# Halves of k and v that add up in the DMA, weight forms at other places, and another order in the opening of a pooled-attention and mixture-of-experts kernel

## The chip, the core and the metric

The kernel runs on one core of one Trainium2 chip. The metric is the device time of one execution in microseconds (us). The kernel before was run eight times: median 503.4, lowest 502.52, highest 504.22. The engines are named as in the profile: PE is TensorE's matmul and PEld its weight load, DVE is VectorE, ACT is ScalarE, POOL is GpSimd, SP is SyncE.

## The reference

```python
# B, H, S, D = 8, 8, 576, 64; q, k, v: [B, H, S, D]
k_p = k.reshape(B, H, 72, 8, D).mean(axis=3)
v_p = v.reshape(B, H, 72, 8, D).mean(axis=3)
attn = softmax(q @ k_p.T / sqrt(D))          # [B, H, S, 72]
x = (attn @ v_p) as [B * S, H * D]           # 4608 tokens x 512
p = domain_probs / domain_probs.sum(-1)      # 4608 x 4
for e in range(4):                           # w1[e]: 512 x 1024, w2[e]: 1024 x 512
    out += p[:, e:e + 1] * (relu(x @ w1[e]) @ w2[e])
```

Inputs and output are f32; the kernel computes in bf16 and sums in f32.

## The kernel before

The tokens are cut into nine chunks. Chunk `c` from 0 to 7 holds the first 512 tokens of batch `c`, in four rows of 128 (a token is `4 p + r` with partition `p` and row `r`); chunk 8 holds the last 64 tokens of all eight batches. Each chunk passes through four experts, so there are 36 steps (c, e), counted by `s`. A step's up product (hidden values, into `H_sb`) runs beside the down product of the step before (into `acc`). Every engine's instructions stand in the order in which the code issues them (`manual_schedule`); nothing reorders them. SP issues the DMA transposes and the stores, POOL all loads. Since an engine works its list from the top, an instruction that waits holds all behind it.

**Forms.** A 2 x 2 block product is made of seven products instead of eight, in the up products from step 2 on (but for step 4) and in the down products from (1, 0) to (8, 2). It needs sums and differences of blocks: `combine_w1` makes those of w1 (L621 to L624) and `combine_w2` those of w2 (L656 to L659, three into `w2_t`, profile name `w_t`, each from the one before, and one in place), four each for an expert; `forms_of` makes four of the chunk's input (L637, L641, `xf`), and `sums_of` four of the hidden values (L733 to L736, `h_s`; the last on POOL). They are additions of 128 x 1024 or 128 x 512 bf16 elements from SBUF to SBUF, on DVE except where a call names `nc.gpsimd`. `relu_sum` (L716) and `add` (L774) read PSUM on DVE; `relu` (L719), `keep` (L712) and the copies L811 and L827 are ACT's. `product` (L668) and `half_of` (L790) are PE's up and down products with forms, `up_half` (L699), `up_plain` (L686; its ReLU on ACT is L690) and `down` (L884) those without. Step 4, the first of chunk 1, is `up_plain` for all eight pieces, with `sums_of` behind it.

**Placing.** `point()` counts places in the order of work and runs what stands in `placed` under its count; `slot()` takes the next piece of `forms_due` and then calls `point()`. Forms of weights stand in `forms_due` by step, with `nothing` for free slots. Attention of batch 1 stands at points 41 to 69 (`second_attention`, within chunk 0), that of batch `b = c + 1` at points of chunk `c` (`attention(c)`).

**Keys and values.** 72 partitions hold 8 rows of 64 for each of 8 heads; they are folded to one row by additions. Batches 1 and 2 are loaded whole (`load_k`, `load_v`, by `load_kv`, L88), k into `raw_kv`, v into the part of `w2_t` that belongs to experts 2 and 3; folding takes a first addition of 4 rows (L222 in `first` for batch 2), one of 2 rows (L227) and a last one (L230; two for keys, to `kp`). From batch 3 on they come as two halves of four rows into `raw_kv` (`load_half`, L95): the second half is added to the first by the DMA, and so it may be issued only when the first has landed; the first addition falls away. `pool_waits` (L252) is a one-element copy on POOL that holds POOL's list until its operand is there; it is set ahead of a load that overwrites what DVE still reads.

**Opening.** Loads are issued as k, half of q0 (rows 0 and 1), v, the other half of q0, w1(0), w2(0) and so on. In `attention_first` PE pools k and v by matmuls (`first_keys`, `first_values`), transposes q (`first_queries`), takes scores (`first_scores`), the context of a pair of rows and half of the heads at a time (`context_first` and `divide`, L393 and L394), and turns it into `xT` (`turn_first`). `warm(n)` issues n matmuls on zeros whose result nobody reads. `attention_rest` places rows 2 and 3 between the first `up_half`s.

**Loads up to 90 us, in POOL's order.** ..., w1(3), w2(2) whole (two DMAs), q(1) as two halves of heads, v(1), w2(3), q_rem(0), q_rem(1); at point 43 k(2), at 52 q(2) and q_rem(2); at point 60 `pool_waits` on the folded v(1), then v(2) and the four forms of w2(1) on POOL:

```python
placed.setdefault(60, []).extend(
    [lambda: pool_waits(vps[1][0:1, H - 1, 0:1]), lambda: load_v(2)]
    + combine_w2(1, nc.gpsimd))
```

The forms of w2(2) stand in `forms_due` of steps 5 and 6 (two in each), those of w2(3) in steps 6 and 7 (one and three). Forms of w2(2) and w2(3) can't be made before v(2) has been folded, since the raw v lies in their place.

Of the kernel before, what the change touches and what calls it, by code (L numbers as in the profile page):

```python
# [18 lines left out]
def kernel(  # L19
# [99 lines left out]
    def load_first_q(half):  # L119
        if half == 0:  # L120
            raws[("q", 0)] = qpool.tile([P, H, NR, D], BF16, name="q_sb")
        nc.gpsimd.dma_start(
            out=raws[("q", 0)][:, :, 2 * half:2 * half + 2, :],
            in_=q[0, :, 0:NT, :].rearrange("h (p r) d -> p h r d", r=NR)[:, :, 2 * half:2 * half + 2],
        )

    def load_q_halves(b):
        raws[("q", b)] = qpool.tile([P, H, NR, D], BF16, name="q_sb")
        for hs in halves:
            nc.gpsimd.dma_start(  # L130
                out=raws[("q", b)][:, hs].rearrange("p h r d -> p h (r d)"),
                in_=q[b, hs, 0:NT, :].rearrange("h (p r) d -> p h (r d)", r=NR),
            )
# [24 lines left out]

    def load_w2(e):
        rows = moe_w2[e].rearrange("(fc p) d -> p fc d", p=P)  # L160
        for lo in (0, FCH // 2):
            fcs = slice(lo, lo + FCH // 2)
            nc.gpsimd.dma_start(out=w2_bf[:, e, fcs], in_=rows[:, fcs])
# [54 lines left out]
    def fold_parts(nm, b, hs, last, engine):  # L218

        def first():  # L220
            raw = raws[(nm, b)]
            engine.tensor_add(out=raw[:, hs, 0:4, :], in0=raw[:, hs, 0:4, :],  # L222
                                 in1=raw[:, hs, 4:8, :])

# [7 lines left out]
        return [first, rest] if b == 2 else [rest]  # L232
# [75 lines left out]
    def first_queries(half):  # L308
        if half == 0:
            state[("qT", 0)] = apool.tile([P, H, 2, P], BF16, name="qT", bufs=1)  # L310
        for g in range(2):
            qt_ps = psum_o.tile([P, 2, 2, P], BF16, tag="o_ps", name="qt_ps")
            for i in range(2):
                h = 2 * (2 * g + i)
                for rr in range(2):
                    for hh in range(2):
                        nc.tensor.transpose(
                            qt_ps[hh * D:(hh + 1) * D, i, rr, :],
                            raws[("q", 0)][:, h + hh, 2 * half + rr, :], ident[:],
                        )  # L320
            copy = nc.scalar.copy if half else nc.vector.tensor_copy
            copy(out=state[("qT", 0)][:, 4 * g + half:4 * g + 4:2], in_=qt_ps[:])
# [21 lines left out]
    def first_scores(half, g):  # L344
        kpT, qT = state[("kpT", 0)], state[("qT", 0)]
        if (half, g) == (0, 0):
            new_exp(0)
        apart = g == 1
        if apart:
            pool, tag = ((psum_h, "h_ps"), (psum_o, "o_ps"))[half]  # L350
            each = [pool.tile([P, NT], F32, tag=tag, name="one") for _ in range(2)]
            each = [bank[:] for bank in each]
        else:
            two = two_banks()
            each = [two[:, hh] for hh in range(2)]
        for i in range(2):
            pair = 2 * g + i
            for hh in range(2):
                lo = hh * D
                nc.tensor.matmul(  # L360
                    each[hh][0:SP, i * TH:(i + 1) * TH], lhsT=kpT[lo:lo + D, 2 * pair, 0:SP],
                    rhs=qT[lo:lo + D, 2 * pair + half].rearrange("c r p -> c (r p)"),
                )
        dst = state[("expT", 0)][:, 4 * g:4 * g + 4, half].rearrange(
            "j (i h) s p -> j h i (s p)", h=2)
        if apart:
            for hh in range(2):
                nc.scalar.activation(
                    out=dst[:, hh], in_=each[hh][0:SP].rearrange("j (i n) -> j i n", i=2),
                    func=ACT.Exp, scale=EXP_SCALE)  # L370
        else:
            nc.scalar.activation(
                out=dst, in_=two[0:SP].rearrange("j h (i n) -> j h i n", i=2),
                func=ACT.Exp, scale=EXP_SCALE)
# [15 lines left out]
    def divide(banks, x_tok):  # L390
        c_ps = banks[:, :, 0:NPAIR * (D + 1)].rearrange("p a (h d) -> p a h d", h=NPAIR)
        inv = npool.tile([P, 2, NPAIR], F32, name="inv")
        nc.vector.reciprocal(out=inv[:], in_=c_ps[:, :, :, D])  # L393
        nc.vector.tensor_tensor(  # L394
            out=x_tok, in0=c_ps[:, :, :, 0:D],
            in1=inv[:].unsqueeze(3).to_broadcast([P, 2, NPAIR, D]), op=ALU.mult,
# [19 lines left out]
    def context_first(t, half):  # L416
        x_tok = h_s[:, t].rearrange("p a n -> p (a n)").rearrange(
            "p (r a h d) -> p r a h d", r=2, a=2, h=NPAIR)
        banks = two_banks()
        for rr in range(2):  # L420
            context_half(0, 2 * t + rr, half, banks[:, rr])
        divide(banks, x_tok[:, :, half])
# [9 lines left out]
    def turn_first(t, half):  # L432
# [8 lines left out]
        copy = nc.vector.tensor_copy if half else nc.scalar.copy  # L441
# [61 lines left out]
    def attention_first():  # L503
# [5 lines left out]
        warm(1)  # L509
        first_queries(0)  # L510
        warm(1)
        first_scores(0, 0)
        warm(1)
        first_scores(0, 1)
        warm(1)
        first_values(0)
        warm(1)
        context_first(0, 0)
# [585 lines left out]
```

The softmax here doesn't subtract the row's maximum and nothing guards it: scores larger than these inputs give would overflow.

## Time and profile before

| | us |
|---|---|
| median of eight runs | 503.4 |
| the profiled execution | 503.38 |
| its span in the profile | 501.7 |
| PE busy | 490.8 (98% of the span) |
| DVE busy | 362.0 (72%) |
| ACT busy | 290.0 (58%) |
| POOL busy | 196.2 (39%) |
| moved by DMA | 41.90 MB, mean 84 GB/s |

The span goes from the first to the last instruction of one profiled execution; the device time contains 1.68 us more. In the lines below L12 is line 12 of the kernel; `out<-in` are the program's names of tiles, followed by partitions x elements. In lines of single instructions the first number is the start in us from the start of the span, the second the duration, and the bracket tells how long the engine had stood idle and what released it. PE's busy time includes `warm` and the pipelining of matmuls, so a busy PE need not be doing needed work.

### The profile page before, as it was taken

How to read it: one execution, taken by the hardware profiler on the slowest of the kernel's cores; microseconds unless marked ns; L12 is line 12 of the kernel's file. 1: busy time of each engine (PE TensorE's matmuls, PEld its weight loads, DVE VectorE, ACT ScalarE, POOL GpSimd, SP SyncE). 2: the span in 40 equal slices, each digit the busy share in tenths (PEclk: the TensorE clock that was granted, in tenths of full speed). 3: DMA queues.
4: the chain of work that ended last, by engine and by line, in shares of the span. 5: the costliest groups of instructions: out<-in, count | busy, mean ns of one | idle time of the engine just before them, and what ended most of it. 6: DMA issues, size and time to landing. Idle time of an engine off the chain costs nothing.

```text
span 501.7 us, 11093 instructions
## 1 busy us (share of the span) xinstructions
PE 490.8 (98%) x4537; PEld 397.5 (79%) x4547; DVE 362.0 (72%) x651; ACT 290.0 (58%) x541; POOL 196.2 (39%) x177
## 2 busy tenths in 40 slices
PE   8999999999999999999999999999999999999996
PEld 3746654797788888888788888887888888888884
DVE  1377885899987767777777777777777767776674
ACT  3654434765666567665766576666665565556650
POOL 8473370458323562267126722661115111512110
PEclk9999999999999999999999999999999999999999
DMA  9999997683925374836573287433310110012003
GB/s 126 205 205 205 202 174 170 77 104 49 131 65 93 47 76 105 109 48 64 107 119 49 23 137 87 68 39 63 65 22 1 54 43 12 1 43 64 2 1 84
DMA packets 84770, 41.90 MB, mean 84 GB/s; under 512 B 48736, under 2 KB 80224, under 8 KB 84720
## 3 DMA queue, kind: packets, MB, share of 16 engines
q0 software_dynamic: 43216, 22.91, 36.4%
q1 hardware_dynamic: 41104, 17.77, 16.9%
q8 instruction: 35, 0.57, 0.5%
q10 hardware_dynamic: 400, 0.52, 0.3%
q14 instruction: 15, 0.12, 0.1%
HBM read 45.69 MB, written 9.44 MB: 110 GB/s over the span
## 4 chain that ended last, share of the span: by engine, by line
PE 81%; DMA 10%; DVE 5%; POOL 2%; issue 1%; ACT 1%; POOLq 0%; ACTq 0%
PE u_ps L790 37%; PE g_ps L668 37%; DMA w_bf<-in_moe_w_dram 5%; DMA q_sb<-in_q_dram 3%; PE o_ps L884 2%; PE two L280 2%; PE h_ps L686 1%; PE two L403 1%; DMA H_sb<-in_v_dram 1%; DVE acc L774 1%; DMA xT<-x_tok 1%; POOL w_bf L154 1%; DVE x_tok L394 1%; DVE H_sb L716 1%; DVE w_t L656 0%
## 5 line engine op out<-in xcount | busy, mean ns | idle before, releaser
L668 PEld LDWEIGHTS <-w_bf 128*128 128x128 bf16 x1848 | 178.6, 98 | 26.4 <-issue 1.3
L774 DVE SCALAR_TENSOR_TENSOR acc<-u_ps,p_all,acc 128x512 f32<-128x512 f32 (+1 forms) x216 | 127.6, 592 | 70.2 <-ACT u_ps L827 65.9
L736 POOL TENSOR_TENSOR h_s<-H_sb,h_s 128x1024 bf16<-128x1024 bf16 x31 | 66.0, 2128 | 241.4 <-DVE h_s L735 228.2
L668 PE MATMUL g_ps<-xT,w_bf 128*128 128x256 bf16 x928 | 129.9, 273 | 0.0
L668 PE MATMUL g_ps<-xf,w_bf 128*128 128x256 bf16 x792 | 109.3, 272 | 0.6 <-DVE H_sb L716 0.2
L790 PEld LDWEIGHTS <-H_sb 128*128 128x128 bf16 x992 | 92.5, 98 | 20.1 <-issue 6.0
L712 ACT COPY r<-g_ps 128x512 f32<-128x512 f32 x136 | 79.7, 586 | 41.1 <-PE g_ps L668 34.0
L790 PE MATMUL u_ps<-w_bf,H_sb 128*128 128x256 bf16 x744 | 102.0, 273 | 0.0
L716 DVE CUSTOM_DVE_ANT_0 H_sb<-g_ps,r 128x512 bf16<-128x512 f32 x136 | 93.5, 688 | 2.8 <-ACT r L712 2.5
L719 ACT ACTIVATE H_sb<-g_ps 128x512 bf16<-128x512 f32 x128 | 76.3, 597 | 18.6 <-PE g_ps L668 18.2
L790 PEld LDWEIGHTS <-h_s 128*128 128x128 bf16 x744 | 72.8, 98 | 8.4
L811 ACT COPY g_ps<-g_ps 128x512 f32<-128x512 f32 x62 | 35.4, 570 | 73.5 <-PE g_ps L668 73.5
L790 PE MATMUL u_ps<-w_t,h_s 128*128 128x256 bf16 x496 | 74.4, 273 | 0.0
L827 ACT COPY u_ps<-u_ps 128x256 f32<-128x256 f32 x62 | 22.2, 358 | 34.1 <-PE u_ps L790 33.7
L790 PE MATMUL u_ps<-w_t,H_sb 128*128 128x256 bf16 x248 | 37.3, 273 | 1.3 <-DVE acc L774 1.3
L790 PE MATMUL u_ps<-w_bf,h_s 128*128 128x256 bf16 x248 | 37.2, 273 | 0.0
L884 PE MATMUL o_ps<-w_bf,H_sb 128*128 128x512 bf16 x145 | 35.6, 379 | 0.5 <-issue 0.2
L284 ACT ACTIVATE expT<-two 72x1024 bf16<-72x1024 f32 x28 | 28.5, 1016 | 0.0
L829 DVE TENSOR_SCALAR acc<-u_ps,p_all 128x512 f32<-128x512 f32 x16 | 12.0, 750 | 19.5 <-ACT u_ps L827 19.5
L884 PEld LDWEIGHTS <-H_sb 128*128 128x128 bf16 x152 | 14.3, 98 | 14.1 <-issue 0.8
L733 DVE TENSOR_TENSOR h_s<-H_sb 128x1024 bf16<-128x1024 bf16 x31 | 21.1, 681 | 2.7 <-ACT H_sb L690 2.7
L394 DVE TENSOR_TENSOR x_tok<-two,inv 128x512 bf16<-128x512 f32 x32 | 22.1, 691 | 1.1
(125 smaller groups left out, 446.8 us busy)
## 6 DMA issues: line engine op xcount, KB each, us to landing
out_dram<-acc SPq DMA_DIRECT2D x32, 256.0 KB, 2.4
w_bf<-in_moe_w_dram POOLq DMA_DIRECT2D x17, 256.0 KB, 8.9
w_bf<-in_moe_w_dram POOLq DMA_DIRECT2D x8, 512.0 KB, 14.6
q_sb<-in_q_dram POOLq DMA_DIRECT2D x6, 512.0 KB, 10.0
raw_kv<-in_k_dram POOLq DMA_DIRECT2D x10, 288.0 KB, 6.8
raw_kv<-in_v_dram POOLq DMA_DIRECT2D x10, 288.0 KB, 6.1
raw_kv<-in_k_dram POOLq DMA_DIRECT2D x2, 576.0 KB, 15.6
w_t<-in_v_dram POOLq DMA_DIRECT2D x2, 576.0 KB, 12.8
```

Source lines behind the costliest of these rows:

```text
L284: nc.scalar.activation(out=state[("expT", b)][:, 2 * pair:2 * pair + 2].rearrange("j h r s p -> j s (h r) p"), in_=two[0:SP].rearrange("j ...
L394: nc.vector.tensor_tensor(out=x_tok, in0=c_ps[:, :, :, 0:D], in1=inv[:].unsqueeze(3).to_broadcast([P, 2, NPAIR, D]), op=ALU.mult,)
L668: nc.tensor.matmul(bank[:, t, :], lhsT=w1_bf[:, e, block, kc, lo:lo + P], rhs=x[:, kc, :], start=(first and t == 0 and kc == 0), stop=(t = ...
L712: nc.scalar.copy(out=r[:], in_=ps[:])
L716: nc.vector._custom_dve(TENSOR_ADD_SAT, out=out, in0=ps[:], in1=r[:], s0=BIG, s1=0.0)
L719: nc.scalar.activation(out=out, in_=ps[:], func=ACT.Relu)
L736: lambda: nc.gpsimd.tensor_sub(out=s4, in0=a12, in1=s2),
L774: nc.vector.scalar_tensor_tensor(out=acc, in0=ps, scalar=prob, in1=acc, op0=ALU.mult, op1=ALU.add,)
L790: nc.tensor.matmul(out, lhsT=lhs[0][:, lhs[1] + f, lhs[2]], rhs=rhs[0][:, rhs[1] + f, rhs[2]], start=(start and f == 0), stop=(f == FCH // ...
L811: nc.scalar.copy(out=s[:], in_=g[:])
L827: nc.scalar.copy(out=two[:, hi], in_=one[:, lo])
L884: nc.tensor.matmul(sums[r][:], lhsT=hidden[(c, e)][:, fc, r * P:(r + 1) * P], rhs=w2_bf[:, e, fc, :], start=(fc == 0), stop=(fc == FCH - 1),)
```

## The change

Four things are changed.

1. *Opening.* q0 is loaded as two halves of the heads (all four rows of a partition: runs of 1 KB read and 512 bytes written, where rows 0 and 1 alone make runs of 512 and 256 bytes), and both halves go ahead of v. Queries and scores are taken by pair of heads. Contexts of rows 0, 1 and 2 are divided one at a time for the first half of the heads (`context_first`), rows 0 and 1 together for the second (`context_two`). Rows 2 and 3 are no longer placed between the `up_half`s, except for their `turn_first`. The eight `up_half`s run both token halves with the first half of w1(0)'s columns first. `warm` has 21 matmuls instead of 23 in the opening.
2. *Loads before 60 us.* The halves of q(1) go between and behind the halves of w2(2).
3. *k(2) and v(2)* are loaded as adding halves into `raw_kv`: k's first half at point 43; at point 60, behind `pool_waits`, k's second half, v's first half, the four forms of w2(1), v's second half. `first` is gone from the folds, and v(2) no longer lies in `w2_t`.
4. *Forms.* The four forms of w2(2) move to `attention(1)`, at the place where the keys of batch 2 have been folded (n = 7); those of w2(3) to slots of steps 5 (one), 6 (two) and 7 (one). The folds of v(2) come one place later.

```diff
             raws[("q", 0)] = qpool.tile([P, H, NR, D], BF16, name="q_sb")
+        hs = halves[half]
         nc.gpsimd.dma_start(
-            out=raws[("q", 0)][:, :, 2 * half:2 * half + 2, :],
-            in_=q[0, :, 0:NT, :].rearrange("h (p r) d -> p h r d", r=NR)[:, :, 2 * half:2 * half + 2],
-        )
-
-    def load_q_halves(b):
-        raws[("q", b)] = qpool.tile([P, H, NR, D], BF16, name="q_sb")
-        for hs in halves:
-            nc.gpsimd.dma_start(
-                out=raws[("q", b)][:, hs].rearrange("p h r d -> p h (r d)"),
-                in_=q[b, hs, 0:NT, :].rearrange("h (p r) d -> p h (r d)", r=NR),
-            )
+            out=raws[("q", 0)][:, hs].rearrange("p h r d -> p h (r d)"),
+            in_=q[0, hs, 0:NT, :].rearrange("h (p r) d -> p h (r d)", r=NR),
+        )
+
+    def load_q_half(b, half):
+        if half == 0:
+            raws[("q", b)] = qpool.tile([P, H, NR, D], BF16, name="q_sb")
+        hs = halves[half]
+        nc.gpsimd.dma_start(
+            out=raws[("q", b)][:, hs].rearrange("p h r d -> p h (r d)"),
+            in_=q[b, hs, 0:NT, :].rearrange("h (p r) d -> p h (r d)", r=NR),
+        )

...
+    def load_w2_half(e, half):
+        rows = moe_w2[e].rearrange("(fc p) d -> p fc d", p=P)
+        fcs = slice(half * FCH // 2, (half + 1) * FCH // 2)
+        nc.gpsimd.dma_start(out=w2_bf[:, e, fcs], in_=rows[:, fcs])
+
...
-        rows = moe_w2[e].rearrange("(fc p) d -> p fc d", p=P)
-        for lo in (0, FCH // 2):
-            fcs = slice(lo, lo + FCH // 2)
-            nc.gpsimd.dma_start(out=w2_bf[:, e, fcs], in_=rows[:, fcs])
+        for half in range(2):
+            load_w2_half(e, half)
...
-        def first():
-            raw = raws[(nm, b)]
-            engine.tensor_add(out=raw[:, hs, 0:4, :], in0=raw[:, hs, 0:4, :],
-                                 in1=raw[:, hs, 4:8, :])
-
-        return [first, rest] if b == 2 else [rest]
+        return [rest]
...
-    def first_queries(half):
-        if half == 0:
+    def first_queries(pair):
+        if pair == 0:
...
-        for g in range(2):
-            qt_ps = psum_o.tile([P, 2, 2, P], BF16, tag="o_ps", name="qt_ps")
-            for i in range(2):
-                h = 2 * (2 * g + i)
-                for rr in range(2):
-                    for hh in range(2):
-                        nc.tensor.transpose(
-                            qt_ps[hh * D:(hh + 1) * D, i, rr, :],
-                            raws[("q", 0)][:, h + hh, 2 * half + rr, :], ident[:],
-                        )
-            copy = nc.scalar.copy if half else nc.vector.tensor_copy
-            copy(out=state[("qT", 0)][:, 4 * g + half:4 * g + 4:2], in_=qt_ps[:])
+        qt_ps = psum_o.tile([P, NR, P], BF16, tag="o_ps", name="qt_ps")
+        for r in range(NR):
+            for hh in range(2):
+                nc.tensor.transpose(
+                    qt_ps[hh * D:(hh + 1) * D, r, :], raws[("q", 0)][:, 2 * pair + hh, r, :],
+                    ident[:],
+                )
+        nc.vector.tensor_copy(
+            out=state[("qT", 0)][:, 2 * pair:2 * pair + 2].rearrange("c h r p -> c (h r) p"),
+            in_=qt_ps[:],
+        )
...
-    def first_scores(half, g):
...
+    def first_scores(pair):
         kpT, qT = state[("kpT", 0)], state[("qT", 0)]
+        if pair == 0:
             new_exp(0)
+        if pair % 2:
+            each = [psum_h.tile([P, NT], F32, tag="h_ps", name="one") for _ in range(2)]
             each = [bank[:] for bank in each]
         else:
             two = two_banks()
             each = [two[:, hh] for hh in range(2)]
+        for hh in range(2):
+            lo = hh * D
+            nc.tensor.matmul(
+                each[hh][0:SP], lhsT=kpT[lo:lo + D, 2 * pair, 0:SP],
+                rhs=qT[lo:lo + D, 2 * pair:2 * pair + 2].rearrange("c h r p -> c (h r p)"),
+            )
+        dst = state[("expT", 0)][:, 2 * pair:2 * pair + 2].rearrange("j h r s p -> j h (r s p)")
+        if pair % 2:
             for hh in range(2):
+                nc.scalar.activation(out=dst[:, hh], in_=each[hh][0:SP], func=ACT.Exp,
+                                     scale=EXP_SCALE)
         else:
+            nc.scalar.activation(out=dst, in_=two[0:SP], func=ACT.Exp, scale=EXP_SCALE)
...
+        n = x_tok.shape[1]
...
-        inv = npool.tile([P, 2, NPAIR], F32, name="inv")
-        nc.vector.reciprocal(out=inv[:], in_=c_ps[:, :, :, D])
+        inv = npool.tile([P, 2, NPAIR], F32, name="inv")[:, 0:n]
+        nc.vector.reciprocal(out=inv, in_=c_ps[:, :, :, D])
...
-            in1=inv[:].unsqueeze(3).to_broadcast([P, 2, NPAIR, D]), op=ALU.mult,
+            in1=inv.unsqueeze(3).to_broadcast([P, n, NPAIR, D]), op=ALU.mult,
...
-    def context_first(t, half):
-        x_tok = h_s[:, t].rearrange("p a n -> p (a n)").rearrange(
+    def first_rows(t):
+        return h_s[:, t].rearrange("p a n -> p (a n)").rearrange(
...
+
+    def context_first(r, half):
+        bank = one_bank(r)
+        context_half(0, r, half, bank)
+        divide(bank[:].unsqueeze(1), first_rows(r // 2)[:, r % 2:r % 2 + 1, half])
+
+    def context_two(t, half):
...
-        divide(banks, x_tok[:, :, half])
+        divide(banks, first_rows(t)[:, :, half])
...
-        copy = nc.vector.tensor_copy if half else nc.scalar.copy
+        copy = nc.vector.tensor_copy if t and half else nc.scalar.copy
...
-        warm(1)
+        warm(3)
...
-        warm(1)
-        first_scores(0, 0)
-        warm(1)
-        first_scores(0, 1)
-        warm(1)
+        for pair in range(1, NPAIR):
+            first_queries(pair)
+            first_scores(pair - 1)
...
-        warm(1)
+        first_scores(NPAIR - 1)
...
+        context_first(1, 0)
...
-        warm(1)
+        context_first(2, 0)
...
-        context_first(0, 1)
-        first_queries(1)
+        context_two(0, 1)
+        context_first(3, 0)
...
-        first_scores(1, 0)
-        first_scores(1, 1)
-
-    def attention_rest():
-
-        return {
-            0: [lambda: context_first(1, 0)],
-            1: [lambda: context_first(1, 1), lambda: turn_first(1, 0)],
-            2: [lambda: turn_first(1, 1)],
-            3: [],
-        }
+        context_first(2, 1)
+        context_first(3, 1)
+        warm(1)
...
             41: [lambda: fold_keys(1, lo)],
-            43: [lambda: fold_keys(1, hi), lambda: load_k(2)],
+            43: [lambda: fold_keys(1, hi), lambda: load_half(2, k, "kraw", 0)],
             47: [second_keys],
...
             add(4, lambda: queries(b))
-            add(6, *key_parts(b)[:2])
-            add(7, *key_parts(b)[2:])
-            add(7, lambda: keys(b))
+            add(6, *key_parts(b)[:1])
+            add(7, *key_parts(b)[1:])
+            add(7, lambda: keys(b), *combine_w2(2))
             add(8, lambda: pool_waits(state[("kpT", b)][0:1, 0, 0:1]))
...
             for n, part in enumerate(value_parts(b)):
-                add(9 + n, part)
+                add(10 + n, part)
             mixed = (16, 18, 20, 21)
...
         )
-        load_first_q(0)
+        for half in range(2):
+            load_first_q(half)
         make_identity(nc, ident[:])
...
             load_first(v, "v", hs)
-        load_first_q(1)
         load_w1(0)
...
         load_w1(3)
-        load_w2(2)
-        load_q_halves(1)
+        for half in range(2):
+            load_w2_half(2, half)
+            load_q_half(1, half)
         load_v(1)
...
                 placed.setdefault(60, []).extend(
-                    [lambda: pool_waits(vps[1][0:1, H - 1, 0:1]), lambda: load_v(2)]
-                    + combine_w2(1, nc.gpsimd))
+                    [lambda: pool_waits(vps[1][0:1, H - 1, 0:1]), lambda: load_half(2, k, "kraw", 1),
+                     lambda: load_half(2, v, "vraw", 0)] + combine_w2(1, nc.gpsimd)
+                    + [lambda: load_half(2, v, "vraw", 1)])
             if s == 1:
...
                 x[3]()
-                w2f = combine_w2(2)
-                forms_due.extend(nothing[:3] + u[3:] + w2f[:1] + nothing[:2] + w2f[1:2])
+                v3 = combine_w2(3)
+                forms_due.extend(nothing[:3] + u[3:] + v3[:1])
             elif s == 6:
-                v3 = combine_w2(3)
-                forms_due.extend(nothing[:3] + w2f[2:] + nothing[:2] + v3[:1])
+                forms_due.extend(nothing[:3] + v3[3:] + v3[1:2])
             elif s == 7:
-                forms_due.extend(nothing[:3] + v3[3:] + v3[1:2] + nothing[:2] + v3[2:3])
+                forms_due.extend(nothing[:3] + v3[2:3])
             elif s == E * B + 1:
...
                 elif s == 0:
-                    for i in range(4):
-                        up_half(j, i)
-                        if j == 0:
-                            for piece in attention_rest()[i]:
-                                piece()
-                        if j == 1 and i == 0:
+                    for n, (t, i) in enumerate(((0, 0), (0, 1), (1, 0), (1, 1))):
+                        up_half(t, 2 * j + i)
+                        if (j, n) == (0, 0):
+                            turn_first(1, 0)
+                        elif (j, n) == (0, 1):
+                            turn_first(1, 1)
                             norm_probs()
-                        between(j, i)
+                        between(j, n)
                 elif s == 1:
```

More of the change, by code (lines that the diff above doesn't have):

```diff
@@ L342, in second_queries @@
         nc.vector.tensor_copy(out=state[("qT", 1)][:, hs], in_=qt_ps[:])
-    def first_scores(half, g):
+    def first_scores(pair):
         kpT, qT = state[("kpT", 0)], state[("qT", 0)]
-        if (half, g) == (0, 0):
+        if pair == 0:
             new_exp(0)
[L348 to L351, printed above, removed]
+        if pair % 2:
+            each = [psum_h.tile([P, NT], F32, tag="h_ps", name="one") for _ in range(2)]
             each = [bank[:] for bank in each]
@@ L355, in first_scores @@
             each = [two[:, hh] for hh in range(2)]
-        for i in range(2):
-            pair = 2 * g + i
-            for hh in range(2):
[L359 to L362, printed above, removed]
-                )
[L364 to L370, printed above, removed]
-        else:
-            nc.scalar.activation(
-                out=dst, in_=two[0:SP].rearrange("j h (i n) -> j h i n", i=2),
-                func=ACT.Exp, scale=EXP_SCALE)
+        for hh in range(2):
[6 more added lines that the diff above has]
+        if pair % 2:
+            for hh in range(2):
+                nc.scalar.activation(out=dst[:, hh], in_=each[hh][0:SP], func=ACT.Exp,
+                                     scale=EXP_SCALE)
+        else:
+            nc.scalar.activation(out=dst, in_=two[0:SP], func=ACT.Exp, scale=EXP_SCALE)
     def first_values(half):
```

## The prediction

> **What bounds the kernel now.** I read the waits of TensorE (PE) first, then the busy time by stage, then the timeline round each wait. TensorE's granted clock is 1.00 in every stage before the last, so a time can only change where PE stands idle or runs its filler, `warm`. The waits of PE (us in total, times, longest):
>
> ```profile
> PE u_ps L790 <- DVE acc L774: 1.3, 2, 0.8
> ...
> PE one L380 <- DMA H_sb<-in_v_dram: 0.8, 1, 0.8
> PE h_ps L686 <- DMA xT<-x_tok: 0.6, 1, 0.6
> ...
> PE qt_ps L338 <- DMA q_sb<-in_q_dram: 0.4, 1, 0.4
> ...
> PE g_ps L668 <- DVE H_sb L716: 0.2, 1, 0.2
> ```
>
> Behind the opening these are all that can be won: 0.40 us at 56.3 (second half of the answer below), 0.64 at 78.6, 0.21 at 93.9, and 0.82 and 0.50 at 119.7 and 133.7. Busy time by stage (PE, PEld, DVE, ACT, POOL, granted clock, DMA share, GB/s) says which engine is short there:
>
> ```profile
> 17.20:56.00 38.80, 38.25 (x267) 23.88 (x267) 26.70 (x52) 21.09 (x35) 18.11 (x25) 1.00 1.26 205
> 56.00:78.00 22.00, 21.29 (x162) 11.83 (x165) 15.89 (x29) 7.20 (x10) 11.37 (x9) 1.00 1.43 192
> ...
> 93.00:135.00 42.00, 40.46 (x410) 34.06 (x408) 39.83 (x67) 25.60 (x48) 23.87 (x20) 1.00 0.83 93
> 135.00:490.00 355.00, 354.64 (x3411) 306.83 (x3410) 259.77 (x464) 220.23 (x421) 125.74 (x97) 1.00 0.36 59
> ```
>
> Until 78 us the loads run at a steady 190 to 205 GB/s; from 93 to 135 VectorE (DVE) is busy 39.83 of 42 us and makes PE wait; from 135 on nothing is left. The timeline shows why DVE is short:
>
> ```profile
> 116.32 2.11 POOL L736 TENSOR_TENSOR h_s<-H_sb,h_s 128x1024 bf16<-128x1024 bf16 x1 [1.22 <-DVE h_s L735]
> 116.74 2.24 DVE L656 TENSOR_TENSOR w_t<-w_bf 128x1024 bf16<-128x1024 bf16 x1
> ...
> 119.70 0.60 PE L790 MATMUL u_ps<-w_t,H_sb 128*128 128x256 bf16 x4 [0.82 <-DVE acc L774]
> ```
>
> L656 takes 0.68 us when GpSimd (POOL) rests and 2.24 here: it stood until POOL's L736 ended (118.43) and then ran 0.55. The same happened to L657 (1.64) and L658 (2.23), while DVE's readers of PSUM (L394, L774, L716) kept their 0.69, 0.75 and 0.68 us beside POOL. So a DVE step from SBUF to SBUF waits out the POOL step it meets, and POOL's next step waits in turn (L637 at 118.40: 1.59 instead of 1.16). This decides my forecast.
>
> **The change part by part.** The profiled execution took 503.38 us, 1.68 more than its span of 501.7; the median is 503.4, so the sum against one stands for the other.
>
> *Opening.* The loads land in the order of issue: k at 5.74 and 7.12, q's first half 8.72, v 11.88 and 13.15, q's second half 14.57, the first piece of w1(0) 15.86. The halves of q0 took 1.60 and 1.42 us; batch 1's halves, whose rows are twice as long, 1.37 and 1.31 (54.88 to 56.25 to 57.56). With batch 1's form q0 costs 2.68 instead of 3.02, so all behind v lands 0.34 us earlier, but v itself, now behind both q halves, lands later: first half 11.88 + 1.34 - 0.23 = 13.0, second 14.57 - 0.34 = 14.2. The Trainium skill ("DMA: Bandwidth & Descriptors", Specifications) puts line rate at 512 bytes and over, and the old q halves have 256-byte runs; if those cost double, the saving would be about 1.4 us by that page, an estimate that the rows do not bear out.
>
> Transposes and scores of the second q half (16 transposes 0.64, scores 0.8) go ahead of v, where PE ran filler. Behind v: values 0.82 and the copy 0.42 bring the first context to 14.35; DVE divides three single rows (half the width of 0.21 + 0.69, with fixed cost about 0.6 each), waits for ACT's copy of the second vp, and divides a pair (0.93) until 17.6; transposes 0.3 and ACT's copy 0.59 let the first up_half start at 18.6 (before: 17.27). Eight up_halves of 0.87, two turns of 0.25 and 0.5 of waiting for the last xT copy end at 26.6, against 26.25: +0.4, between -0.3 (v lands at 12.3) and +0.8. Two `warm` fewer lie in the waiting and count zero.
>
> *q(1) between the halves of w2(2).* q's first half lands near 53.3 instead of 56.25, so the 0.40 us at 56.3 goes; the second lands at 57.2 and PE wants it at 57.6 - 0.4 + 0.4 = 57.6. w2(2)'s second half, now at 55.9, is first read at 58.2. PE stands level at 57.6; better than -0.36 it cannot be.
>
> *k(2) and v(2) as halves.* POOL before and the accumulate's model later on:
>
> ```profile
> 65.97 0.18 POOL L252 COPY mark<-vp 1x1 bf16<-1x1 bf16 x1 [5.78 <-DVE vp L257]
> 66.20 0.85 POOL L88 DMA_DIRECT2D w_t<-in_v_dram  x1
> 67.07 2.14 POOL L656 TENSOR_TENSOR w_t<-w_bf 128x1024 bf16<-128x1024 bf16 x1
> ...
> 73.57 2.12 POOL L659 TENSOR_TENSOR w_bf<-w_bf 128x1024 bf16<-128x1024 bf16 x1
> 99.83 1.40 POOL L95 DMA_DIRECT2D raw_kv<-in_k_dram  x1 [6.33 <-DMA raw_kv<-in_k_dram]
> ```
>
> The last line is what comes: an adding half may not be issued before the first half has landed, and POOL stands (6.33 us there). k(2)'s first half lands behind q_rem (68.22 - 0.34 = 67.9) plus 2.0 (the half issued at 92.67 landed 2.0 behind q_rem: 97.53 to 99.54), at 69.9. Queued behind that wait on POOL: k's second half (1.40), v's first (0.85), the four weight forms of expert 1 (8.6 us before, 67.07 to 75.7), v's second half. So the forms end at 69.9 + 1.4 + 0.85 + 8.6 = 80.8 instead of 75.7. Their own readers come after 100 us; the cost lies on DVE:
>
> ```profile
> 78.62 0.42 DVE L637 TENSOR_TENSOR xf<-xT 128x512 bf16<-128x512 bf16 x1 [1.56 <-DMA xT<-x_tok]
> ...
> 83.16 0.49 DVE L230 TENSOR_TENSOR kp<-raw_kv 72x256 bf16<-72x256 bf16 x2
> 86.37 0.69 DVE L733 TENSOR_TENSOR h_s<-H_sb 128x1024 bf16<-128x1024 bf16 x1 [2.72 <-ACT H_sb L690]
> ```
>
> L637 is an SBUF step and now meets POOL's third or fourth form; it or the fold behind it is held until 80.8 + 0.5 = 81.3. From the fold to the last kp took 83.65 - 79.68 = 3.97; without the inner L222 (0.72) 3.25. Then four forms of expert 2, three of them each on the one before, 0.72 + 0.73 + 0.61 + 0.68 = 2.74 (as at 35.43 to 38.2). L733 starts at 81.3 + 6.0 = 87.3 instead of 86.37, and PE waited for L734 with nothing to spare at 87.84 (half 7 reads it). So PE stands +0.95 there whatever it did before, as long as the last xT lands before about 79.7; the opening's +0.4 or -0.36 and the 0.64 at 78.6 are swallowed. kpT: kp is ready at 84.5 instead of 83.65 and 2.7 (issue 83.68, landed 86.41) puts it at 87.2 to 87.8; scores want it at 87.5 to 88.4: no more. Bounds: half landed at 69.3 and issue 0.86 give -0.2; 70.6 and one more POOL step between gives +1.7.
>
> The skill ("DMA: Bandwidth & Descriptors", Anatomy of one DMA) gives each DMA about 2.0 us of fixed cost, which would speak against two more of them with some 4 us. In this full queue pieces of 256 KB land 1.29 apart and of 512 KB 2.53 (17.12, 18.41, 19.70, 22.23): no fixed part shows, and I take none.
>
> *DVE's list from 91 to 135.* Gone: two L222 (0.72, 0.68), L657 at 102.39 (0.68), and of the four w_t steps at 116.74 to 130.73 (2.24, 0.80, 1.64, 2.23) three move to slots where 0.68 stood and one takes the place of 0.80. The waits 0.21, 0.82 and 0.50 then have no cause: -1.53; at worst -0.8, if a moved form meets POOL's key fold at 108.84.
>
> Sum: +0.95 - 1.53 = -0.6, from 503.38 to **502.8 us**; own range -1.7 to +0.5, 501.7 to 503.9.
>
> **The rivals.** *Clean win.* POOL's forms end before 79.85, or xT lands so that DVE meets none of them: then +0.95 is 0, and the opening's bound (-0.36) and some 0.3 of the xT wait stay won: -1.53 - 0.36 - 0.3 = -2.2, 501.2. For it: 1.3 us of uncertainty in the landing. Against it: the POOL sum needs 0.9 less.
>
> *Slower: transposes behind the adding loads, at L686.* xT's four transposes are issued 69 to 75. One issued at 103.98 beside an adding half (99.83 to 108.78) landed at 109.02, one of 148.89 beside one that landed at 153.22 landed at 153.85. If k's second half takes 9.0 us as at 99.83 it lands at 79.0, v's first half 2.0 later, the last transpose 1.0 behind: 82.0, and PE starts L686 3.5 later than at 78.64; less 1.53, +2.0: 505.4. It decides from a last xT later than 81.0. Against it: 6.4 us (146.78 to 153.22) is the commoner row and gives about 79.
>
> *The relief is not one.* A moved form meets POOL again near 109 and only 0.2 of the 1.53 is won: +0.75, 504.1.
>
> **How the numbers follow.** Forecast 0.50, clean win 0.23, transposes 0.17, no relief 0.10. About 0.2% (1.0 us) is what a measurement here tells from no change: faster than 502.4 are the clean win (0.23) and 0.15 of the forecast, slower than 504.4 are 0.14 of the transposes, 0.05 of the last and 0.01 of the forecast: 0.38, 0.42, 0.20. The range leaves out the ends of both outer rivals: 501.0 to 504.9.
>
> **What would show it.** Right: POOL waits some 4 us near 66 to 70; its L646 to L649 end near 81; DVE's first xf or fold takes about 2 us; PE waits about 1 us at half 7 near 88; no PE wait on DVE's acc at 119 and 133. Wrong: forms ending by 79.9 with no long DVE step (clean win), PE idle over 2 us before L676 (transposes), or a DVE form over 1.5 us between 94 and 135 with PE waiting behind.

## The result and the profile after

| | us | ratio to before, 95% interval |
|---|---|---|
| before, 32 runs | 503.33 (502.52 to 505.22) | |
| after, 11 runs | 506.13 (504.5 to 507.59) | 1.0054 (1.0044 to 1.0063) |
| after, the profiled execution | 503.98, span 502.2 | |

After is slower by 2.8 us. The forecast was a gain, 502.8 us with a range of 501.0 to 504.9; the time moved the other way and lies above the range. Already this table holds a warning: the profiled execution took 503.98 us, faster than all eleven timed ones. What the profile shows can explain 0.6 us of the loss (503.98 against 503.38), and 2.15 us (506.13 less 503.98) must come from something that it does not show. Every execution has on record its mean granted clock of TensorE (1.000 is full speed): 1.000 in the profiled one, 0.997 in three runs (504.5 to 505.8), 0.991 or 0.992 in the other eight (505.52 to 507.59).

First what the profile shows. The waits of PE in after (line numbers are about ten lower there: L676 is the old L686, `up_plain`; L780 the old L790):

```profile
PE h_ps L676 <- DMA xT<-x_tok: 4.1, 1, 4.1
...
PE qt_ps L337 <- DMA q_sb<-in_q_dram: 0.5, 1, 0.5
PE u_ps L780 <- DVE H_sb L724: 0.3, 1, 0.3
```

The two waits on DVE's `acc` near 119 and 133 us (0.82 and 0.50) are gone, as forecast. The wait for xT has grown from 0.64 to 4.07 us. The busy time by stage (PE, PEld, DVE, ACT, POOL, granted clock, DMA share, GB/s) says the same:

```profile
56.00:78.00 22.00, 20.56 (x153) 10.95 (x153) 15.38 (x29) 7.20 (x10) 10.94 (x9) 1.00 1.21 144
78.00:93.00 15.00, 11.39 (x72) 6.67 (x74) 8.72 (x19) 7.67 (x14) 4.50 (x3) 1.00 0.87 161
93.00:135.00 42.00, 41.68 (x427) 35.30 (x425) 36.06 (x65) 26.74 (x51) 25.32 (x24) 1.00 0.79 88
135.00:490.00 355.00, 355.00 (x3415) 307.04 (x3415) 259.89 (x464) 220.85 (x423) 125.81 (x98) 1.00 0.38 59
```

From 93 to 135 DVE is busy 36.06 us instead of 39.83, and PE 41.68 instead of 40.46. From 56 to 78 the transfers fall from 192 to 144 GB/s. The timeline round the long wait:

```profile
68.66 1.42 POOL L95 DMA_DIRECT2D raw_kv<-in_k_dram  x1 [3.02 <-DMA raw_kv<-in_k_dram]
68.69 6.00 SPq L424 DMA_TRANSPOSE xT<-x_tok  x3
...
69.55 1.39 POOL L95 DMA_DIRECT2D raw_kv<-in_v_dram  x1
...
70.40 2.69 POOL L646 TENSOR_TENSOR w_t<-w_bf 128x1024 bf16<-128x1024 bf16 x1
...
75.38 1.37 SPq L424 DMA_TRANSPOSE xT<-x_tok  x1
...
77.45 2.11 POOL L649 TENSOR_TENSOR w_bf<-w_bf 128x1024 bf16<-128x1024 bf16 x1
...
81.55 0.43 DVE L627 TENSOR_TENSOR xf<-xT 128x512 bf16<-128x512 bf16 x1 [5.00 <-DMA xT<-x_tok]
81.56 7.07 PE L676 MATMUL h_ps<-xT,w_bf 128*128 128x512 bf16 x31 [4.07 <-DMA xT<-x_tok]
```

k(2)'s adding half is issued in the same moment as the first transpose of xT (68.66 and 68.69), and v(2)'s first half stands behind it. The trace also has the time at which each transfer has landed: k's adding half at 75.76, v's half at 80.04, and the last three transposes at 80.12, 80.41 and 81.43, the first of these 0.08 us behind v's half. SP issued the last of them at 75.38, only 0.29 later than before (75.09), when it landed at 78.50. So SP's instruction list is not the cause; the transposes wait in the DMA.

Starts of the same matmul of PE in both profiles give the account of the profiled execution (a minus means that after is ahead):

| PE in before, us | what | after less before |
|---|---|---|
| 27.33 | opening done | -0.52 |
| 73.25 | context of batch 1 | -0.51 |
| 78.64 | `up_plain` of step 4 | +2.93 |
| 114.15 | | +2.55 |
| 139.85 | | +1.08 |
| 497.31 | last matmul | +0.54 |

### The profile page after: what moved, and what is told of

Same layout as the page of the kernel before. It is cut to its first block, busy times and chain, and to the rows that moved or that the text cites. A ratio compares the mean times of both kernels' runs of the same rounds, so it can differ in the third digit from the quotient of the medians.

```text
span 502.2 us, 11076 instructions
## 1 busy us (share of the span) xinstructions
PE 488.4 (97%) x4526; PEld 397.0 (79%) x4537; DVE 358.0 (71%) x654; ACT 289.5 (58%) x540; POOL 197.9 (39%) x179
## 4 chain that ended last, share of the span: by engine, by line
PE 85%; DMA 9%; POOL 3%; DVE 1%; issue 1%; ACT 0%; POOLq 0%
PE u_ps L780 38%; PE g_ps L658 38%; DMA raw_kv<-in_k_dram 3%; DMA w_bf<-in_moe_w_dram 3%; DMA q_sb<-in_q_dram 3%; PE o_ps L874 3%; PE two L280 2%; PE two L395 1%; PE h_ps L676 1%; DMA xT<-x_tok 1%; POOL w_bf L156 1%; POOL H_sb L107 1%; POOL w_bf L164 0%; DVE acc L764 0%; PE o_ps L889 0%
## 5 line engine op out<-in xcount | busy, mean ns | idle before, releaser
L780 PEld LDWEIGHTS <-H_sb 128*128 128x128 bf16 x992 | 92.2, 98 | 19.6 <-DVE H_sb L724 4.6
L702 ACT COPY r<-g_ps 128x512 f32<-128x512 f32 x136 | 79.7, 586 | 40.1 <-PE g_ps L658 33.0
L780 PE MATMUL u_ps<-w_bf,H_sb 128*128 128x256 bf16 x744 | 102.0, 273 | 0.3 <-DVE H_sb L724 0.3
L780 PEld LDWEIGHTS <-h_s 128*128 128x128 bf16 x744 | 72.8, 98 | 8.4
L780 PE MATMUL u_ps<-w_t,h_s 128*128 128x256 bf16 x496 | 74.4, 273 | 0.0
L780 PE MATMUL u_ps<-w_t,H_sb 128*128 128x256 bf16 x248 | 37.3, 273 | 0.0
L780 PE MATMUL u_ps<-w_bf,h_s 128*128 128x256 bf16 x248 | 37.2, 273 | 0.0
```

The costliest lines, as they stand in the source:

```text
L702: nc.scalar.copy(out=r[:], in_=ps[:])
L780: nc.tensor.matmul(out, lhsT=lhs[0][:, lhs[1] + f, lhs[2]], rhs=rhs[0][:, rhs[1] + f, rhs[2]], start=(start and f == 0), stop=(f == FCH // ...
```

## The experiments

My theory after the result, called A below: one wait of 4 us for the transposes costs 3.4 us, the moved forms give 1.8 back, and the idle time makes the granted clock fall behind it, which the profiled execution happened to escape. The rivals are named with each run. The first four:

**e1_opening** leaves k(2), v(2) and the forms as before, and keeps the rest of the change (the diff is against after):

```diff
-            43: [lambda: fold_keys(1, hi), lambda: load_half(2, k, "kraw", 0)],
+            43: [lambda: fold_keys(1, hi), lambda: load_k(2)],
...
-                    [lambda: pool_waits(vps[1][0:1, H - 1, 0:1]), lambda: load_half(2, k, "kraw", 1),
-                     lambda: load_half(2, v, "vraw", 0)] + combine_w2(1, nc.gpsimd)
-                    + [lambda: load_half(2, v, "vraw", 1)])
+                    [lambda: pool_waits(vps[1][0:1, H - 1, 0:1]), lambda: load_v(2)]
+                    + combine_w2(1, nc.gpsimd))
...
```

> The opening and the order of q(1) and w2(2) alone, with k(2), v(2) and the forms as before. In the profile of after PE ran 0.52 us ahead of before from 22 us to 78 us. Theory A (the loss comes from one long wait of PE at half 78 us, for the transposes of xT, and from a lower granted clock behind it): this kernel has no such wait (0.6 to 1.2 us there, as before), its clock stays at 0.999 or 1.0, and 0.1 to 0.5 us are won: 502.8 to 503.2. Rival B (the opening itself lowers the clock in the runs without a profile): clock near 0.992 and 504.5 or more.

Measured: 502.68 us, ratio 0.9990 (0.9976 to 1.0005); clock 0.998 or higher in ten of twelve runs. PE waits 0.61 for xT, and 0.22, 0.82 and 0.51 later on, as before. The opening and the order of q(1) cost nothing; by the medians they win 0.8 us, which the interval does not tell from nothing. A low clock is the exception here (two runs, 0.990 and 0.993), where in after it is the rule, so B (the opening lowers the clock) is out as the cause of after's loss. What lowered the clock in these two runs was not traced; two of before's 17 runs beside e9 below also had 0.992 and 0.993, so the clock can fall without the long wait too.

**e2_halves** is the other part alone: before, with the adding halves and the moved forms (the diff is against before):

```diff
-            43: [lambda: fold_keys(1, hi), lambda: load_k(2)],
+            43: [lambda: fold_keys(1, hi), lambda: load_half(2, k, "kraw", 0)],
...
-            add(7, lambda: keys(b))
+            add(7, lambda: keys(b), *combine_w2(2))
...
-                    [lambda: pool_waits(vps[1][0:1, H - 1, 0:1]), lambda: load_v(2)]
-                    + combine_w2(1, nc.gpsimd))
+                    [lambda: pool_waits(vps[1][0:1, H - 1, 0:1]), lambda: load_half(2, k, "kraw", 1),
+                     lambda: load_half(2, v, "vraw", 0)] + combine_w2(1, nc.gpsimd)
+                    + [lambda: load_half(2, v, "vraw", 1)])
...
```

> The halves of k(2) and v(2) and the moved forms alone, with the opening of before. A: PE waits 3.5 to 4.2 us for xT near 78 us, gets 1.8 us back between 93 and 135 us, and the clock falls to about 0.992 in the runs: 503.3 + 3.4 - 1.8 + 2.2 = 507.1, between 506 and 507.5. B: the wait, but no lower clock: 504.9.

Measured: 506.43 us, ratio 1.0063 (1.0042 to 1.0084). PE stood from 78.00 to 81.91. This profile was taken in an execution of 507.46 us, and it shows what the profile of after had not. The busy time in pieces of 2 us (columns as above; the clock is the number ahead of the DMA share):

```profile
78.00:80.00 2.00, 0.00 (x0) 0.00 (x0) 0.00 (x0) 0.00 (x0) 2.00 (x2) 1.00 1.41 150
80.00:82.00 2.00, 0.09 (x1) 0.12 (x2) 0.10 (x1) 0.00 (x0) 1.67 (x2) 0.59 1.10 351
82.00:84.00 2.00, 2.00 (x6) 0.62 (x6) 1.97 (x6) 0.19 (x1) 0.06 (x1) 0.50 1.29 257
84.00:86.00 2.00, 2.00 (x6) 0.75 (x5) 1.93 (x6) 0.89 (x2) 0.00 (x0) 0.50 1.19 141
86.00:88.00 2.00, 2.00 (x8) 0.80 (x7) 1.93 (x4) 0.71 (x2) 0.00 (x0) 0.71 1.05 207
```

PE is busy again from 81.91 and does 6 matmuls in 2 us; in the kernel of e3 below it does 9 to 11. The trace's clock record has only 1.0 and 0.5, and 0.5 from 80.34 to 87.17, 6.8 us, as the pieces say (1.64 + 4 + 1.16). PE worked in some 5.2 of them, so 2.6 us of work were lost. A mean clock of 0.993 over a span of 505.8 is a lack of 3.5 us, which is half of 7. So this part of the change alone brings the whole loss.

**e3_filled** puts 18 matmuls on zeros into the place in PE's list where after waits:

```diff
                     if j:
+                        warm(18)
                         up_plain(c, e, range(FCH))
```

> After, with 18 matmuls on zeros (some 3.9 us) on PE in the place of the wait for xT. Nothing becomes ready earlier. A (the idle time lowers the clock, and the clock costs the part of the loss that the profiled run at clock 1.0 does not show, 506.13 - 503.98 = 2.15 us): clock 1.0 in the runs and 504.0 to 504.4. B (the clock falls for another reason): 506.1 and clock 0.992.

Measured: 503.74 us, ratio 1.0011 (1.0002 to 1.0020); eleven of twelve clocks at 0.998 or higher. PE ran `warm` to 81.53 and then waited 0.56 more for the same late transposes, and the clock stayed at 1.00 behind them:

```profile
78.00:82.00 4.00, 3.53 (x17) 1.39 (x15) 0.00 (x0) 0.00 (x0) 3.31 (x2) 1.00 1.20 240
82.00:84.00 2.00, 1.91 (x9) 0.91 (x10) 1.89 (x6) 0.60 (x1) 0.00 (x0) 1.00 1.29 267
```

Work that nobody reads makes the kernel 2.4 us faster: the time that the profile of after did not show is the clock behind the idle time.

**e4_v_early**, against after, takes v(2)'s first half out of the way of the transposes:

```diff
-            43: [lambda: fold_keys(1, hi), lambda: load_half(2, k, "kraw", 0)],
+            43: [lambda: fold_keys(1, hi), lambda: load_half(2, k, "kraw", 0),
+                 lambda: load_half(2, v, "vraw", 0)],
...
-                     lambda: load_half(2, v, "vraw", 0)] + combine_w2(1, nc.gpsimd)
...
```

> After, with v(2)'s first half issued at point 43 right behind k(2)'s first half, so that only k's adding half and the transposes share the DMA near 70 to 80 us. A1 (v's first half, queued behind k's adding half, holds the transposes): the last xT lands near 79 instead of 81.4, PE waits 1 to 1.7 us, the clock stays at 1.0, and DVE's first xf may meet a form on POOL as the prediction said (up to +1): 501.2 to 502.4. A2 (the adding half alone holds them): the wait stays over 3 us, 505 or more.

Measured: 504.34 us, ratio 1.0013 (1.0000 to 1.0026). The last xT landed at 79.11 and PE waited 1.41, as A1 (v's first half, behind k's adding half, holds the transposes) has it; but the time is 2 us over what I expected. The timeline and two pieces of the busy time show what came in between:

```profile
79.23 1.12 DVE L628 TENSOR_TENSOR xf<-xT 128x512 bf16<-128x512 bf16 x1 [2.33 <-DMA xT<-x_tok]
79.25 7.07 PE L677 MATMUL h_ps<-xT,w_bf 128*128 128x512 bf16 x31 [1.41 <-DMA xT<-x_tok]
80.01 1.39 POOL L95 DMA_DIRECT2D raw_kv<-in_v_dram  x1
...
83.55 3.09 SPq L245 DMA_TRANSPOSE kpT<-kp  x1
...
90.22 0.47 PE L280 MATMUL two<-qT,kpT 64*72 64x256 bf16 x4 [2.06 <-DMA kpT<-kp]
```

```profile
90.00:92.00 2.00, 1.78 (x11) 1.16 (x12) 0.00 (x0) 1.02 (x1) 2.00 (x3) 0.61 0.00 0
92.00:94.00 2.00, 2.00 (x12) 1.44 (x11) 0.21 (x1) 0.36 (x1) 1.90 (x3) 0.54 0.38 27
```

v(2)'s adding half, issued at 80.01, stands beside the keys' transposes: they land at 90.18 (86.41 in before), 0.58 behind the adding half (89.60). In after this was there too (kpT landed at 89.85), but PE came 2 us later and did not wait for it. Behind the 2.06 us of waiting stand 3.4 us of half clock (1.56 + 1.84). The first line shows the forecast's own mechanism: `xf` met POOL's last form (77.96 to 80.07) and took 1.12 us, where it took 0.42 in before.

The next three ask whether the adding is at fault, whether kpT can be freed, and whether the gain needs the adding at all.

**e5_overwrite**, against after, leaves the sum out: the second halves of batch 2 overwrite the first.

```diff
-            accum_op=ALU.add if half else ALU.bypass,
+            accum_op=ALU.add if half and b > 2 else ALU.bypass,
```

> After, with the second halves of k(2) and v(2) written over the first instead of added to them: the same bytes, issues and waits, and the sum of two halves of batch 2 left out. If the adding itself is what is slow (6 to 7 us for 288 KB, where a plain half of that size took about 2 in the full queue), k's second half lands near 72, v's first half near 75, the last xT near 78.5 to 79, PE waits 1 to 1.5 us instead of 4.07, the clock stays up, and the time is 501.5 to 502.8. If it is only that two more DMAs stand in the queue, the wait stays over 3 us and the time over 505.

Measured: 501.53 us, ratio 0.9963 (0.9945 to 0.9982). The waits of PE:

```profile
PE h_ps L676 <- DMA xT<-x_tok: 1.9, 1, 1.9
...
PE two L280 <- DMA kpT<-kp: 0.9, 1, 0.9
```

So the adding makes 2.2 of the 4.07 us, and 1.25 more (1.89 less before's 0.64) are there without it, with two halves that before does not have in this place. Where the adding acts is not where I expected: k's second half itself landed 5.3 us after its issue ended, and 5.7 when adding; but v's plain half behind it landed 1.94 later instead of 4.28. Waiting for the load ahead is not peculiar to adding: here too the second transpose landed just behind v's half (77.56 and 77.07).

**e7_v_apart** starts from e4 and moves v(2)'s adding half behind the keys' transposes, the folds of v(2) later:

```diff
-                    + combine_w2(1, nc.gpsimd) + [lambda: load_half(2, v, "vraw", 1)])
+                    + combine_w2(1, nc.gpsimd))
...
+            add(8, lambda: load_half(2, v, "vraw", 1))
             add(8, lambda: (load_q(b + 1), load_q_rem(b + 1)))
...
-                add(10 + n, part)
+                add(13 + n, part)
```

> As the kernel with v(2)'s first half at point 43, and besides v(2)'s adding half behind the wait for the keys' transposes (attention(1), n = 8, ahead of q(3)), and the folds of v(2) three places later. In the kernel with the early half PE waited 2.06 us at 88 for kpT, whose transposes were issued beside v's adding half, and the clock fell to 0.54 to 0.61 from 90 to 94. If an adding half holds whatever transposes stand beside it, that wait goes (kpT near 86.5), the clock stays at 1.0, and only the 1.4 us at 78 and some wait for v's folds are left: 501.3 to 502.8. If kpT is late because its fold comes late on DVE, the wait stays and the time is near 504.

Measured: 504.51 us, ratio 1.0025 (1.0004 to 1.0047). kpT landed at 85.33 and nobody waited for it, as expected; but the time was missed by 2 us. POOL's timeline:

```profile
89.95 1.33 POOL L95 DMA_DIRECT2D raw_kv<-in_v_dram  x1
90.82 1.39 POOL L113 DMA_DIRECT2D q_sb<-in_q_dram  x1
...
103.76 1.40 POOL L95 DMA_DIRECT2D raw_kv<-in_k_dram  x1 [10.00 <-DMA raw_kv<-in_k_dram]
104.63 2.68 POOL L728 TENSOR_TENSOR h_s<-H_sb,h_s 128x1024 bf16<-128x1024 bf16 x1
```

q(3) and k(3)'s first half now stand behind the adding half, which landed at 103.47 instead of 99.54 (before). POOL stood 10.0 us for it, and POOL's piece of `sums_of` (L728), queued behind that wait, came late for PE (1.41 us at 106). The profiled execution took 502.87 us, other executions at clock 1.000 took 503.68 to 504.44, and three at 0.995 took 506.9 to 508.1; what made these three slower was not traced and stays open.

**e8_home**, against e1, gives the forms their new places without any adding half of batch 2. Raw v takes 8 of the 12 KB that a partition has for the forms of experts 2 and 3; put at the other end, it leaves the first two of expert 2's three places of `w2_t` free:

```diff
-        wide = (w2_t[0:SP, 2:4].rearrange("p a b f d -> p (a b f d)")[:, 0:H * POOL * D] if nm == "vraw"
+        wide = (w2_t[0:SP, 2:4].rearrange("p a b f d -> p (a b f d)")[:, -H * POOL * D:] if nm == "vraw"
...
-            add(7, lambda: keys(b))
+            w2f.extend(combine_w2(2))
+            add(7, lambda: keys(b), w2f[0], w2f[1], w2f[3])
...
-                w2f = combine_w2(2)
-                forms_due.extend(nothing[:3] + u[3:] + w2f[:1] + nothing[:2] + w2f[1:2])
...
+                forms_due.extend(nothing[:3] + u[3:] + v3[:1] + nothing[:2] + w2f[2:3])
...
+                forms_due.extend(nothing[:3] + v3[3:] + v3[1:2])
...
+                forms_due.extend(nothing[:3] + v3[2:3])
```

> No adding halves for batch 2: the opening alone (502.68), with raw v at the other end of its part of w2_t, so that it leaves the first two of expert 2's three places free. Three forms of w2(2) then move to attention(1), n = 7, the fourth to step 5, and those of w2(3) as in after. If the gain of after from 93 to 135 us (1.8 us) comes from the places of the forms alone and not from the dropped first additions, the waits of 0.22, 0.83 and 0.51 go here too, and the wait for xT stays near 0.6: 500.9 to 501.5. If it comes from the dropped additions, two of the waits stay: 502 to 502.7.

Measured: 500.62 us, ratio 0.9931 (0.9907 to 0.9955), clocks 0.999 or 1.000: 3 us faster than before and 5.5 faster than after. The waits of PE, and the stage of DVE:

```profile
PE h_ps L683 <- DMA xT<-x_tok: 0.6, 1, 0.6
PE u_ps L787 <- DVE H_sb L731: 0.4, 1, 0.4
...
PE g_ps L665 <- DVE H_sb L713: 0.2, 1, 0.2
```

```profile
93.00:135.00 42.00, 41.52 (x424) 35.26 (x423) 36.82 (x66) 26.08 (x51) 22.47 (x19) 1.00 0.88 98
```

DVE's load falls from 39.83 (before) to 36.82 with the first additions still in place, and in after it fell to 36.06: the relief is mostly the forms' places, 3.0 of the 3.8 us. PE's matmuls run 1.94 us ahead of e1 from 135 us on, 0.53 of it from an earlier landing of q(1).

**e9_held**, against e8, asks whether idle time alone does it, with no adding half near:

```diff
                     if j:
+                        held_ps = psum_o.tile([P, 2 * P], F32, tag="o_ps", name="o_ps")
+                        nc.tensor.matmul(held_ps[:, 0:P], lhsT=ident[:], rhs=state[("qT", 2)][:, 0, 0, :])
                         up_plain(c, e, range(FCH))
```

> The kernel with raw v at the other end of its part of w2_t (500.62, no adding half of batch 2), with one more matmul ahead of step 4's up_plain that reads the transposed q of batch 2, which landed at 80.82 there: PE stands idle some 3.6 us in one piece instead of 0.60, and nothing else is changed. If idle time of that length lowers the clock by itself, the clock is 0.5 for 4 to 6 us behind it, the mean clock of the runs 0.992 to 0.997, and the time 500.6 + 3.0 + 1.5 to 2.5 = 505.1 to 506.1. If the low clock belongs to the adding transfers, the clock stays at 1.0 and the time is 503.6.

Measured: 506.41 us, ratio 1.0049 (1.0032 to 1.0066). PE stood from 77.51 to 81.12. The wait, and the busy time in pieces of 2 us:

```profile
PE o_ps L1065 <- DMA qT<-q_sb: 3.6, 1, 3.6
```

```profile
78.00:80.00 2.00, 0.00 (x0) 0.00 (x0) 1.40 (x3) 0.00 (x0) 0.00 (x0) 1.00 1.18 308
80.00:82.00 2.00, 0.88 (x5) 0.50 (x6) 1.93 (x7) 0.00 (x0) 0.00 (x0) 0.97 0.65 186
82.00:84.00 2.00, 2.00 (x7) 0.64 (x5) 1.93 (x6) 0.60 (x1) 0.00 (x0) 0.50 0.35 131
84.00:86.00 2.00, 2.00 (x8) 0.82 (x7) 1.50 (x3) 0.90 (x2) 0.00 (x0) 0.67 0.48 82
```

3.0 us more of idle time than in e8 cost 5.8 us by the medians. The one execution at a clock of 1.000 took 503.48 us, 2.9 over e8: there the idle time cost its own length and no more. The half clock lasted 0.12 + 2 + 1.32 = 3.4 us in this execution (505.60 us, mean clock 0.997); the runs at 0.991 to 0.993 took 505.8 to 507.3. By their mean clock and the piece seen in e2, these had about twice as much.

## Why the prediction was wrong

**The likeliest case was chosen wrongly.** The forecast's case, +0.95 from DVE held by POOL's forms, did not occur, because its condition failed: it needed the last xT before about 79.7, and that came at 81.43. (POOL's forms had ended at 79.56.) The rival "transposes behind the adding loads" happened, with its mechanism, its place (L676) and nearly its price: it said k's second half at 79.0, v's 2.0 later, the last transpose at 82.0, and PE 3.5 us later. Measured were 75.76, 4.28 later, 81.43, and a start 2.93 us later (3.43 us more of waiting, since PE came 0.51 earlier). I gave it 0.17, because I took the commoner row, 6.4 us for an adding half, and added 2.0 for the plain half behind it. k's half did take about that time (7.1). The step that failed is the 2.0, which came from a queue of plain loads: behind an adding half and beside transposes the same 288 KB took 4.28, and 1.94 when nothing was added (e5). The profile before already had such a row: v(3)'s adding half landed at 131.69, the 512 KB of q(4) behind it 3.85 us later, where q(1)'s two halves of 256 KB took 2.68 in the plain queue (54.88 to 57.56), and a transpose issued beside them at 125.44 landed only at 135.03.

**The clock was not in the sum at all.** I wrote that the clock is 1.00 in every stage, "so a time can only change where PE stands idle", and priced idle time at its length. That holds for the 0.64 us of before. For 3.6 to 4 us it does not: e9 paid 5.8 us for 3.0, e3 got 2.4 us back without making anything ready sooner. With the clock's 2.15 on top, the rival's 505.4 would have been 507.6. That 505.4 lies near the measured 506.13 is in part luck: it lacks the clock, and against that 1.4 us more that the opening (0.52), the relief (0.32) and the later steps (0.54) won. The Trainium skill ("TensorE: Matmul & The Clock Gate", Part 1 and its table "Why this matters for your kernels") says that idle time of about 3.4 us puts the clock at half and that gaps over some 3 us are to be avoided. The waits of 3.91 us (e2) and 3.61 us (e9) agree, with half clock for 6.8 and 3.4 us behind them. The lower edge differs: in e2 the clock fell 2.34 us after PE had stopped, and in e4 a wait of 2.06 us was enough.

How the profiled execution of after kept 1.00 behind 4.07 us can be inferred from the traces. Within each trace the clock changes only at whole steps of 3.413 us: the stretches at full clock last 75.09 us in e2 and e9 (22 steps) and 85.33 in e4 (25). In the step at whose end the clock fell, PE had been idle for 2.34 us (e2), 2.65 (e9) and 2.06 (e4). Counted from the start of its clock record (4.40), after's profile has the end of a step at 79.50, in the middle of the wait from 77.49 to 81.56. So 2.01 us of it lie in one step and 2.07 in the next, each about the least that was enough elsewhere, and the clock stayed up. By this reading the same wait costs more or less by where it falls on the steps, and the profiled execution was lucky; no run moved a wait along the steps, so it is not shown, nor where the edge lies exactly.

**The other terms.**

- *Opening:* +0.4 forecast, -0.52 measured. v's first half landed at 12.05, not 13.0. I had charged it the whole transfer of q's second half (1.34); but before, v landed 3.16 us behind q's first half, although its second half took only 1.27 more; q's second half (10.19) went into that hole. The prediction's 1.4 us for short runs rested on a factor of two that was my assumption and not the page's; the two halves of q0 took 1.37 and 1.40 us, 0.24 less in all than before.
- *q(1):* it landed at 57.17 against 57.2 forecast; PE came 1.0 earlier, waited 0.52, and stayed 0.5 ahead.
- *POOL:* it waited 3.02 us (some 4 forecast), since k's first half landed at 68.04 and not 69.9; its forms ended at 79.56, not 80.8.
- *Relief:* -1.53 forecast, -1.85 measured (from +2.93 to +1.08).
- *Range:* the worst bounds of the forecast's own terms add up to +0.9 (1.7 less 0.8), not the +0.5 that I gave.
- *DVE beside POOL:* The Trainium skill ("SBUF — State Buffer", Who interferes with whom) has DVE's two-operand steps from SBUF contend with GpSimd's reads; L628 in e4 (1.12 us beside a POOL form, 0.42 in before without one) agrees.
- *A further 0.54 us* were won in small steps from 155 us on, which was not followed up.

With the terms as measured: -0.5 opening, +3.4 wait, -1.85 relief, -0.5 later make +0.5 for the profiled execution; the other 2.15 of the median, put down to the clock, make the rest.

## What to carry to other kernels

When a forecast contains a wait of several us on TensorE, price the clock behind it as well, and compare the profiled execution's clock with those of the timed runs before trusting the profile's account. Here a load that adds in the DMA made the load behind it and the transposes beside it late; before halving a load to free a buffer, look whether another place in the same buffer frees what is needed. If a wait can't be removed, matmuls on zeros in it can be worth more than they cost.

## What was not expected of the hardware

The granted clock went to half behind PE's waits of 3.61 us (e9), 3.91 (e2) and 2.06 (e4), for one or two steps of 3.41 us, in most executions but not in all: by their mean clock, after's twelve had none once, about 3.4 us in three, and more in eight.

An adding half that lands 5.7 us after the end of its issue is hardly slower than the same half overwriting (5.3), yet a plain half of 288 KB behind it took 4.28 us instead of 1.94.

Of the transposes issued while an adding half was under way, the first to land behind it came within 0.7 us of that half or of the load behind it (80.12 behind 80.04, 77.63 behind 76.97, 90.18 behind 89.60). This is no rule: in after the transpose issued together with k's adding half landed ahead of it (72.97), and kpT 1.4 us behind v's adding half (89.85 and 88.45).
